# FFT layer, MLP and soft routing in one kernel: the MLP's second product replaced by turned squares, slot sums of squares and one product at the end

## The chip, the cores and the metric

The kernel runs as one program on one core of a Trainium2 chip. The metric is the device time of the whole program in microseconds (us), the median over several runs; lower is better.

## What is computed

Three layers follow one another over 8 sequences of 3072 tokens with 256 features (24576 tokens). The first filters each sequence in the frequency domain. The second is an MLP with a squared relu and 2048 hidden features. The third is a soft mixture: 32 slots, 4 for each of 8 experts, gather means over all tokens, and each token takes back a mean over the slots.

```python
# attention: X = rfft(x); Y = softshrink(X @ w + b); y = irfft(Y)
h = np.maximum(x @ w_in, 0.0)              # MLP, w_in 256 x 2048
x = h * h @ w_out                          # w_out 2048 x 256
logits = x @ phi                           # 32 slots
d = np.exp(logits - logits.max(0)); d /= d.sum(0) + 1e-09    # over the tokens
slot_input = d.T @ x
slot_out[e] = np.maximum(slot_input[e] @ w1[e], 0.0) @ w2[e]
c = np.exp(logits - logits.max(1)); c /= c.sum(1) + 1e-09    # over the slots
out = c @ slot_out
```

The MLP's output x is used in two places only, the logits and slot_input.

## The kernel before

**The front** (the loop over h that calls first_stage, b_mm, l_mm and c_mm) runs the FFT layer in units u = 0, 1, ... 95 and writes its result to DRAM (zd). Beside it runs decode(), a generator: the MLP's weights come as float64, and 32 pieces of 256 KB are loaded (raw, on the DMA queue of SyncE, SP), turned into float32 by VectorE, ScalarE and GpSimd (v, L389 and L391), and split into a part in fp32r (hi) and the remainder (lo). The loop takes one step of decode() for each h after 16, a second one when h is a multiple of 6, and at u = 80 it takes all that are left in one go (drain, L614).

**The MLP stage** has 32 steps s of 768 tokens, two halves of 384 (TOK). Its input is computed by stage_d(s+1), a generator that runs beside step s: two fills (psY, L442), each of 64 narrow float32 matmuls, then copies and splits (yh, yl). A step has 8 units q, each for 256 hidden features: a unit does seven products by Strassen's scheme as Winograd wrote it, so that four blocks (2 feature blocks a, 2 token halves c; k = 2a + c) come of seven products j and not eight. Each product is three fp32r matmuls of 128x384 (hi*hi, hi*lo, lo*hi, L658) on one of the two PSUM banks psA and psX. ScalarE copies intermediate sums away (r1, V and W, L664), VectorE adds them (h, L669) and squares (g).

The second product belongs to the unit before (prev): second(k), for each of the four blocks, multiplies the square, split again into gh and gl, by w_out, 24 matmuls of 128x384 in a unit (mm3, L116 to L118) on four banks psO that add up over the 8 units of a step:

```python
for m in range(2):
    mm3(po[m, c][:, :TOK], wo[q][:, 0, a, d], wo[q][:, 1, a, d], h, l, ...)
```

evac_o copies psO to xm, the MLP's output with features on partitions.

**The routing** is done by route(r) for a pair of steps, a generator of its own: logits (pl, L731), running maximum nn and factor al (the sums so far are multiplied by al when a larger maximum comes), exponentials e, 24 transposes of xm (px, L739) and six of the scores (py, L749), the means over slots (over_slots), slot sums (pz, L755: 12 float32 matmuls of 256 columns) which are added to acc by VectorE (L829), and a table of weights for the output (pc, co, stored to cd).

**The order of the work** is written out by hand: each engine executes its instructions as the loop issues them (manual_schedule). In a unit, beside(k) stands at four places and takes a step of stage_d where the slot 4q + k is in plan, and a step of route where it is in pairs:

```python
u.product(u.a, 0, True); r1 = u.copy("r1"); u.product(u.x, 1, True); u.add(0, r1)
prev.second(0); ...; u.square(0); beside(0)
u.product(u.a, 5, False); v = u.copy("V"); u.product(u.x, 6, True)
prev.second(3); ...; beside(1)
u.product(u.a, 4, False); u.add(3, u.copy("W")); prev.second(2); ...; beside(2)
u.product(u.a, 2, False); ...; u.product(u.x, 3, False); u.add(2, v)
prev.second(1); beside(3)
```

**The end**: in the last step the buffers of the MLP's weights become free, and loads of the experts' weights follow (load_w1 in free_wo and free_wi). Then come the logits and slot sums of the last step, the combination of the sums over the partitions (p_m, p_s, p_si), the experts (ph L1048, p2o L1066), their output by slots (pso, L1088) and the output stage, which writes the result.

## Time and profile before

| | |
|---|---|
| time, median of 3 runs | 2807.98 us (2805.99 to 2808.20) |
| the profiled execution | 2806.21 us, of which the trace's span is 2804.1 us |
| mean granted clock of TensorE | 0.989 |
| TensorE (PE) busy | 2746.1 us, 98% |
| VectorE (DVE) busy | 2049.3 us, 73% |
| ScalarE (ACT) busy | 1686.6 us, 60% |
| GpSimd (POOL) busy | 178.4 us, 6% |
| moved by DMA | 190.46 MB, mean 68 GB/s |

Busy is the time in which an engine had an instruction at work; matmuls overlap, so that the next one starts before one has ended, and a duration of a matmul is longer than the time that it keeps TensorE from the next. PEld is TensorE's loading of weights, which runs beside its matmuls. A row of the timeline joins successive instructions of one line: start, time to the last end, engine, line, operation, output and inputs, shapes, count. An idle time before an instruction stands in brackets with what ended it.

### The profile page before, as it was taken

How to read it: one execution, taken by the hardware profiler on the slowest of the kernel's cores; microseconds unless marked ns; L12 is line 12 of the kernel's file. 1: busy time of each engine (PE TensorE's matmuls, PEld its weight loads, DVE VectorE, ACT ScalarE, POOL GpSimd, SP SyncE). 2: the span in 40 equal slices, each digit the busy share in tenths (PEclk: the TensorE clock that was granted, in tenths of full speed). 3: DMA queues.
4: the chain of work that ended last, by engine and by line, in shares of the span. 5: the costliest groups of instructions: out<-in, count | busy, mean ns of one | idle time of the engine just before them, and what ended most of it. 6: DMA issues, size and time to landing. Idle time of an engine off the chain costs nothing.

```text
span 2804.1 us, 53515 instructions
## 1 busy us (share of the span) xinstructions
PE 2746.1 (98%) x21255; PEld 2571.1 (92%) x21255; DVE 2049.3 (73%) x4166; ACT 1686.6 (60%) x3720; POOL 178.4 (6%) x236
## 2 busy tenths in 40 slices
PE   7999999999999999999999999999999999999995
PEld 4788879899999999999999999999999999999974
DVE  3677777677777777777777777777777777777764
ACT  2677776566565656565656565656565656565643
POOL 0355441000000000000000000000000000000000
PEclk8999999999999999999999999999999999999997
DMA  8998986300000000000000000000100000000169
GB/s 238 250 247 239 247 218 157 68 12 12 15 13 15 12 15 12 15 12 15 12 15 13 15 12 15 12 15 12 22 12 19 12 15 12 15 12 4 38 236 381
DMA packets 99338, 190.46 MB, mean 68 GB/s; under 512 B 10928, under 2 KB 71728, under 8 KB 93072
## 3 DMA queue, kind: packets, MB, share of 16 engines
q1 hardware_dynamic: 97920, 183.86, 24.0%
q8 instruction: 167, 2.74, 0.4%
q10 hardware_dynamic: 1168, 3.18, 0.3%
q14 instruction: 83, 0.68, 0.1%
HBM read 108.36 MB, written 78.64 MB: 67 GB/s over the span
## 4 chain that ended last, share of the span: by engine, by line
PE 94%; DMA 3%; DVE 1%; issue 1%; SPq 0%; ACT 0%; POOL 0%; ACTq 0%; DVEq 0%; POOLq 0%
PE psA L658 20%; PE psX L658 14%; PE psO L118 13%; PE psO L116 13%; PE psO L117 13%; PE psB L243 3%; PE psC L327 3%; PE psY L442 2%; PE psA L210 2%; PE psL L116 2%; PE psL L117 1%; PE psL L118 1%; PE px L739 1%; DMA out_dram<-ob 1%; PE pz L755 1%; PE pl L731 1%
## 5 line engine op out<-in xcount | busy, mean ns | idle before, releaser
L118 PE MATMUL psO<-gh,wo 128*128 128x384 f32 x2048 | 684.6, 334 | 0.0
L116 PE MATMUL psO<-gh,wo 128*128 128x384 f32 x2048 | 684.0, 334 | 0.0
L117 PE MATMUL psO<-gl,wo 128*128 128x384 f32 x2048 | 684.0, 334 | 0.0
L698 DVE TENSOR_TENSOR gl<-g,gh 128x384 fp32r<-128x384 f32 x1024 | 558.0, 552 | 87.0 <-ACT gh L681 72.9
L116 PEld LDWEIGHTS psO<-gh,wo 128*128 128x128 f32 x2048 | 384.4, 188 | 0.0
L117 PEld LDWEIGHTS psO<-gl,wo 128*128 128x128 f32 x2048 | 384.4, 188 | 0.0
L118 PEld LDWEIGHTS psO<-gh,wo 128*128 128x128 f32 x2048 | 384.4, 188 | 0.0
L658 PE MATMUL psA<-yh,wia 128*128 128x384 f32 x1024 | 350.5, 342 | 0.6 <-ACT W L664 0.6
L658 PE MATMUL psA<-yh,wib 128*128 128x384 f32 x1024 | 350.1, 342 | 0.0
L658 PE MATMUL psX<-yh,wia 128*128 128x384 f32 x1024 | 342.8, 335 | 3.0 <-ACT sc L337 3.0
L669 DVE TENSOR_TENSOR h<-psX,r 128x384 f32<-128x384 f32 x256 | 142.7, 558 | 220.3 <-PE psX L658 215.5
L690 DVE SCALAR_TENSOR_TENSOR g<-h 128x384 f32<-128x384 f32 x512 | 281.8, 550 | 0.1
L664 ACT COPY r<-psA 128x384 f32<-128x384 f32 x256 | 123.4, 482 | 261.0 <-PE psA L658 261.0
L669 DVE TENSOR_TENSOR h<-psX,W 128x384 f32<-128x384 f32 x256 | 142.8, 558 | 184.9 <-ACT W L664 183.3
L674 ACT ACTIVATE r<-psA 128x384 f32<-128x384 f32 x256 | 126.2, 493 | 249.2 <-PE psA L658 249.2
L681 ACT CAST gh<-g 128x384 fp32r<-128x384 f32 x512 | 263.4, 514 | 14.5 <-DVE g L690 12.3
L692 DVE TENSOR_TENSOR g<-r 128x384 f32<-128x384 f32 x512 | 260.2, 550 | 0.1
L683 ACT ACTIVATE gh<-r 128x384 fp32r<-128x384 f32 x512 | 240.7, 518 | 8.1
L664 ACT COPY W<-psA 128x384 f32<-128x384 f32 x256 | 123.4, 482 | 202.7 <-PE psA L658 202.7
L658 PEld LDWEIGHTS psA<-yh,wia 128*128 128x128 f32 x1024 | 192.2, 188 | 13.3 <-issue 10.3
L664 ACT COPY V<-psA 128x384 f32<-128x384 f32 x256 | 123.0, 480 | 126.1 <-PE psA L658 126.1
L658 PEld LDWEIGHTS psX<-yh,wia 128*128 128x128 f32 x1024 | 192.5, 188 | 3.6 <-ACT sc L337 3.3
(213 smaller groups left out, 5091.4 us busy)
## 6 DMA issues: line engine op xcount, KB each, us to landing
bt<-ad SPq DMA_DIRECT2D x96, 256.0 KB, 4.8
zd<-sc SPq DMA_DIRECT2D x96, 256.0 KB, 4.5
zt<-zd SPq DMA_DIRECT2D x64, 384.0 KB, 6.0
xt<-in_x_dram SPq DMA_DIRECT2D x126, 192.0 KB, 4.2
ad<-sa SPq DMA_DIRECT2D x112, 192.0 KB, 4.2
out_dram<-ob SPq DMA_DIRECT2D x21, 1024.0 KB, 19.5
w<-in_moe_w_dram SPq DMA_DIRECT2D x5, 1024.0 KB, 12.6
raw<-in_moe_w_in_dram SPq DMA_DIRECT2D x16, 256.0 KB, 4.8
```

Source lines behind the costliest of these rows:

```text
L116: nc.tensor.matmul(o, lhsT=ah, rhs=bh, start=start, stop=False)
L117: nc.tensor.matmul(o, lhsT=ah, rhs=bl, start=False, stop=False)
L118: nc.tensor.matmul(o, lhsT=al, rhs=bh, start=False, stop=stop)
L658: nc.tensor.matmul(p, lhsT=w[:, k, l], rhs=r[:, j], start=start and n == 0, stop=n == 2, skip_group_check=True)
L664: nc.scalar.copy(t, self.a)
L669: nc.vector.tensor_tensor(out=h, in0=self.x, in1=t, op=ALU.add)
L674: nc.scalar.activation(out=t, in_=self.g[k].pop() if k in self.g else self.a, func=AF.Relu)
L681: nc.scalar.copy(h, self.g[k][0])
L683: nc.scalar.activation(out=h, in_=self.g[k][0], func=AF.Square)
L690: nc.vector.scalar_tensor_tensor(out=g, in0=t, scalar=0.0, in1=t, op0=ALU.max, op1=ALU.mult)
L692: nc.vector.tensor_tensor(out=g, in0=t, in1=t, op=ALU.mult)
L698: nc.vector.tensor_tensor(out=l, in0=g, in1=f(h), op=ALU.subtract)
```

## The change

The product by w_out is taken out of the loop. The squares g of a unit are kept as they are (float32).

- **Logits.** decode() computes pw = w_out phi (2048 x 32) in the front: it stores the float32 w_out to DRAM (wod), transposes the piece (pv), copies it (vt), multiplies by phi (pw) and copies the result. Unit.logits() multiplies pw by the four squares, four float32 matmuls of 32x384 in four column groups of the bank ls, which adds up over the step's units.
- **Turned squares.** Unit.turn(k) transposes a square in three pieces of 128 tokens (psT), and ScalarE copies them into one of 18 granules, in memory that w_out's pieces had (wg) and a new tile (gt).
- **Slot sums.** gather(s, i), for the unit nine places back, multiplies the granules of that unit by the exponentials ee of its step, 12 float32 matmuls of 32x128 in four column groups (into_slots), and VectorE adds the result to acc, which is now 8 blocks of 128 columns, one for each q.
- **Routing by step.** route(s) runs in step s + 1: copy of the scores (scores), sum over the two feature halves by a product with psum2 and the maximum (highest), exponentials, their transposes (weights), total, and the table for the output (rows).
- **The end.** load_wo reads w_out back in step 31; after the last slot sums acc is combined (p_f), multiplied by w_out (p_d) and folded (p_si). Eight of the loads of w1 stand behind the last slot sums now (load_w1(wg[:, k])); free_wo is gone.
- psX has two banks (fresh takes the next), psO none; ls has one and psT, for turns and gathers, two; stage_d has three more yields, so that its steps lie elsewhere, and starts at slot 6 in every step.

```diff
-    wia, wib, wo = [], [], []
+    wia, wib = [], []
+    GR = 3 * 2 * 128
+    wg = wpool.tile([128, 8, 4 * DM], F32, tag="wg", name="wg")
+    wgf = wg.rearrange("p k n -> p (k n)")
+    pw = wgf[:, 10 * GR:10 * GR + 32 * NF].rearrange("p (k n) -> p k n", n=32)
...
             if k:
-                split(wo[q][:, 0], wo[q][:, 1], v, nc.gpsimd)
+                nc.sync.dma_start(out=wod[:, 2 * q:2 * q + 2], in_=v)
+                p = pbank(f"pv{q}").rearrange("p (a d n) -> p a d n", a=2, d=2)
+                for o in range(2):
+                    for dh in range(2):
+                        nc.tensor.transpose(p[:, o, dh], in_=v[:, o, 128 * dh:128 * dh + 128], identity=ident)
+                yield
+                vt = dec.tile([128, 5, 128], F32, tag="s", name=f"vt{q}")[:, :4].rearrange("p (a d) n -> p a d n", a=2)
+                nc.scalar.copy(vt, p)
+                yield
+                p = pbank(f"pw{q}")[:, :64].rearrange("p (a n) -> p a n", a=2)
+                for o in range(2):
+                    for dh in range(2):
+                        nc.tensor.matmul(p[:, o], lhsT=vt[:, o, dh], rhs=phi[:, dh], start=dh == 0, stop=dh == 1)
+                yield
+                nc.scalar.copy(pw[:, 2 * q:2 * q + 2], p)
...
                 nc.scalar.copy(yf[2 * g + dh], ps[g])
+                yield
+            if dh == 0:
                 yield
...
+        lgp = psL.tile([128, 512], F32, tag="l", name="ls")[:, :TOK]
+        NG = 18
+        own = wk.tile([128, NG - 10, GR], F32, tag="gt", name="gt")
+        acc = rt.tile([128, NW, 128], F32, tag="acc", name="acc")
+        nc.vector.memset(acc, 0.0)
...
+        def granule(n, a):
+
+            i = (2 * n + a) % NG
+            t = wgf[:, GR * i:GR * i + GR] if i < 10 else own[:, i - 10]
+            return t.rearrange("p (b q n) -> p b q n", b=2, q=NQ)
...
+            def turn(self, *ks):
+
+                for k in ks:
+                    a, c = divmod(k, 2)
+                    p = psT.tile([128, 512], F32, tag="t", name=f"psT{self.n}_{k}")[:, :TOK].rearrange(
+                        "p (q n) -> p q n", q=NQ)
+                    for j in range(NQ):
+                        nc.tensor.transpose(p[:, j], in_=self.g[k][:, 128 * j:128 * j + 128], identity=ident)
+                    nc.scalar.copy(granule(NW * self.s + self.q, a)[:, c], p)
+
+            def logits(self):
+
+                for k in range(4):
+                    a, c = divmod(k, 2)
+                    o = 32 * (2 * c + a)
+                    nc.tensor.matmul(lgp[o:o + 32], lhsT=pw[:, 2 * self.q + a], rhs=self.g[k], start=self.q == 0,
+                                     stop=self.q == NW - 1, skip_group_check=True)
...
+        def into_slots(s, i, p):
+
+            for q in range(NQ):
+                for c in range(2):
+                    for a in range(2):
+                        o = 32 * (2 * c + a)
+                        nc.tensor.matmul(p[o:o + 32], lhsT=ee[s][:, q, c], rhs=granule(NW * s + i, a)[:, c, q],
+                                         start=q == 0, stop=q == NQ - 1, skip_group_check=True)
+
+        def gather(s, i):
+
+            p = psT.tile([128, 512], F32, tag="t", name=f"pz{s}_{i}")[:, :128]
+            into_slots(s, i, p)
+            nc.vector.scalar_tensor_tensor(out=acc[:, i], in0=acc[:, i], scalar=al[s], in1=p, op0=ALU.mult, op1=ALU.add)
...
+        def scores(s):
+            lw[s] = mid([128, TOK], "lw", s)
+            nc.scalar.copy(lw[s], lgp)
+
+        def highest(s, p):
+            p = p[:, :TOK]
+            nc.tensor.matmul(p, lhsT=psum2, rhs=lw[s], start=True, stop=True)
+            bx = small([128, 1], "bx", s)
+            no, nn = nm[s % 3], nm[(s + 1) % 3]
+            nc.vector.tensor_reduce(out=bx, in_=p, axis=AX.X, op=ALU.max)
...
+        def weights(s, p):
+            p = turn_rows(ew.pop(s), p)
+            ee[s] = rt.tile([128, NQ, 2, 32], F32, tag="ee", name=f"ee{s}", bufs=2)
+            nc.vector.tensor_copy(ee[s], p[:, :, :, 0])
...
+            p = turn_rows(lw.pop(s), p)
+            lt = rt.tile([128, NQ, 64], F32, tag="lt", name=f"lt{s}")
+            nc.vector.tensor_reduce(out=lt.rearrange("p q (b n) -> p q b n", b=2), in_=p.rearrange("p q b a n -> p q b n a"),
+                                    axis=AX.X, op=ALU.add)
...
+        def load_wo():
+            ts = [f(yp[0].tile([128, 7, TOK], F32R, tag=t, name=f"wo_{t}").rearrange("p a n -> p (a n)")) for t in ("yh", "yl")]
+            h = NF // 2
+            for k, t in enumerate(ts):
+                t = t[:, :h * DM].rearrange("p (k d) -> p k d", d=DM)
+                nc.sync.dma_start(t, wod[:, h * k:h * k + h])
...
-        pairs = [(6, 7, 9, 10, 12, 14, 15, 17, 18, 20, 21, 23, 24, 25, 26, 27, 28, 29), (9, 11, 12, 13, 19, 22)]
-        plan = set(range(25))
+        turns = (2, 3, 4, 5, 8, 13, 15, 17, 19, 21, 23, 25, 27)
+        plan = set(range(26))
...
+                if s > 0 and slot == turns[0]:
+                    side["r"] = route(s - 1, bank)
+                if s > 0 and slot in turns:
                     next(side["r"], None)
+                if s == NSB - 1 and slot == 8:
+                    load_wo()
...
             if u:
                 u.product(u.a, 0, True)
                 r1 = u.copy("r1")
-                u.product(u.x, 1, True)
+                u.product(u.fresh(0), 1, True)
                 u.add(0, r1)
             if prev:
-                prev.second(0)
-                prev.relu(2)
-                prev.hi(2)
-                prev.square(2)
-                prev.hi(1)
-                prev.square(1)
+                prev.turn(0)
             if u:
                 u.square(0)
                 beside(0)
                 u.product(u.a, 5, False)
                 v = u.copy("V")
-                u.product(u.x, 6, True)
+                u.product(u.fresh(1), 6, True)
             if prev:
-                prev.lo(2)
-                prev.second(3)
+                prev.turn(3)
             if u:
-                u.hi(0)
-                u.lo(0)
                 beside(1)
                 u.product(u.a, 4, False)
-                u.add(3, u.copy("W"))
+                w = u.copy("W")
             if prev:
-                prev.lo(1)
-                prev.second(2)
-                if prev.q == NW - 1:
-                    evac_o(prev.s, 0)
+                prev.logits()
+            if n > NW and n - 9 < NW * (NSB - 1):
+                gather(*divmod(n - 9, NW))
             if u:
+                u.add(3, w)
                 u.square(3)
                 beside(2)
                 u.product(u.a, 2, False)
                 u.relu(1)
-                u.hi(3)
                 u.product(u.x, 3, False)
+                u.square(1)
                 u.add(2, v)
-                u.lo(3)
+                u.square(2)
             if prev:
-                prev.second(1)
+                prev.turn(1, 2)
                 if prev.s == NSB - 1:
-                    free_wo(prev.q)
-                if prev.q == NW - 1:
-                    evac_o(prev.s, 1)
+                    free_wi(prev.q)
             if u:
                 beside(3)
-                if s == NSB - 1:
-                    free_wi(q)
...
+        pz = [psT.tile([128, 512], F32, tag="t", name=f"pz_{h}").rearrange("p (i n) -> p i n", n=128) for h in range(2)]
+        for i in range(4):
+            into_slots(s, i, pz[0][:, i])
...
+        for i in range(4, NW):
+            into_slots(s, i, pz[1][:, i - 4])
+        for k in range(8):
+            load_w1(wg[:, k])
...
+        lt = rows(s, bank("pr_z"))
+        p = bank("p_f").rearrange("p (i n) -> p i n", n=64)
+        for i in range(NW):
+            nc.tensor.matmul(p[:, i], lhsT=acc[:, i], rhs=mean, start=True, stop=True)
+        sf = [full(t, f"sf_{t}", 1)[:, :256].rearrange("p (i a n) -> p i a n", a=2, n=32) for t in ("V", "W")]
+        for h, copy in enumerate((nc.vector.tensor_copy, nc.scalar.copy)):
+            copy(sf[h].rearrange("p i a n -> p i (a n)"), p[:, 4 * h:4 * h + 4])
+        p = bank_x("p_d")
+        for n in range(NF):
+            i, a = divmod(n, 2)
+            c = n % 4
+            nc.tensor.matmul(p[32 * c:32 * c + 32, :DM], lhsT=sf[i // 4][:, i % 4, a], rhs=wof[n], start=n < 4, stop=n >= NF - 4,
+                             skip_group_check=True)
+        sd = full("r1", "sd", 1)[:, :DM]
+        nc.vector.tensor_copy(sd, p[:, :DM])
+        p = bank_x("p_si")
+        for dh in range(2):
+            nc.tensor.matmul(p[:, 32 * dh:32 * dh + 32], lhsT=sd[:, 128 * dh:128 * dh + 128], rhs=same[:, :32],
+                             start=True, stop=True)
+        nc.vector.tensor_copy(si, p[:, :64].rearrange("p (a s) -> p a s", a=2))
```

The lines of the changed kernel lie some 37 below (L658 is L695, L669 is L706).

**The order on TensorE** in a unit, from the end of product 4 (wib, third part) to the start of the next products; psO, psA and psX are banks, gh and gl the split squares, wia and wib the weights. Before:

```order
L658 MATMUL psA_6_14277<-yh_12793,wib_826 128x384
L116 MATMUL psO_00_13772<-gh_5_2_14297,wo_824 128x384
L117 MATMUL psO_00_13772<-gl_5_2_14324,wo_824 128x384 [waits DVE_49]
L118 MATMUL psO_00_13772<-gh_5_2_14297,wo_824 128x384
L116 MATMUL psO_10_13776<-gh_5_2_14297,wo_824 128x384
L117 MATMUL psO_10_13776<-gl_5_2_14324,wo_824 128x384
L118 MATMUL psO_10_13776<-gh_5_2_14297,wo_824 128x384
L658 MATMUL psA_6_14277<-yh_12793,wia_825 128x384 [waits Activation_49]
L658 MATMUL psA_6_14277<-yl_12794,wia_825 128x384
L658 MATMUL psA_6_14277<-yh_12793,wia_825 128x384
L658 MATMUL psX_6_14278<-yh_12793,wia_825 128x384 [waits DVE_49]
```

Now:

```order
L695 MATMUL psA_3_12846<-yh_11848,wib_806 128x384
L738 MATMUL ls<-g_2_0_12742,wg 32x384
L738 MATMUL ls<-g_2_1_12829,wg 32x384
L738 MATMUL ls<-g_2_2_12833,wg 32x384 [waits DVE_49]
L738 MATMUL ls<-g_2_3_12785,wg 32x384
L759 MATMUL pz_2_12896<-gt,ee_12631 32x128 [waits PE_49]
L759 MATMUL pz_2_12896<-gt,ee_12631 32x128 x11
L695 MATMUL psA_3_12846<-yh_11848,wia_805 128x384 [waits Activation_49]
L695 MATMUL psA_3_12846<-yl_11849,wia_805 128x384
L695 MATMUL psA_3_12846<-yh_11848,wia_805 128x384
L695 MATMUL psX_3_1_12871<-yh_11848,wia_805 128x384 [waits DVE_49]
```

The six matmuls by w_out are gone; the logits of the unit before (ls) and a gather (pz), which waits on a semaphore of TensorE, stand in their place. Product 3 (psX) waits for VectorE before and now.

**The order on VectorE** around h of block 3 (add(3), which reads psX and W). Before:

```order
L698 TENSOR_TENSOR gl_6_0_10924<-g_6_0_10895,gh_6_0_10922 128x384 [waits Activation_49]
L669 TENSOR_TENSOR h_6_3_10933<-psX_6_10868,W_6_10931 128x384 [waits Activation_49]
L698 TENSOR_TENSOR gl_5_1_10935<-g_5_1_10893,gh_5_1_10891 128x384
L690 SCALAR_TENSOR_TENSOR g_6_3_10943<-h_6_3_10933 128x384 [waits DVE_49]
L669 TENSOR_TENSOR h_6_2_10956<-psX_6_10868,V_6_10909 128x384 [waits PE_49]
L698 TENSOR_TENSOR gl_6_3_10958<-g_6_3_10943,gh_6_3_10951 128x384 [waits Activation_49]
```

Now:

```order
L766 SCALAR_TENSOR_TENSOR acc<-acc,al_15045,pz_2_15332 128x128 [waits PE_49]
L706 TENSOR_TENSOR h_3_3_15346<-psX_3_1_15307,W_3_15326 128x384 [waits Activation_49]
L720 SCALAR_TENSOR_TENSOR g_3_3_15348<-h_3_3_15346 128x384 [waits DVE_49]
L470 TENSOR_TENSOR yl_15097<-yf_0_15098,yh_15096 128x384
L718 TENSOR_TENSOR g_3_1_15359<-r_3_1_15354 128x384 [waits Activation_49]
L706 TENSOR_TENSOR h_3_2_15361<-psX_3_1_15307,V_3_15305 128x384 [waits PE_49]
L720 SCALAR_TENSOR_TENSOR g_3_2_15363<-h_3_2_15361 128x384 [waits DVE_49]
```

The update of acc, which waits for TensorE, stands ahead of h 3, and the subtractions that make gl are gone.

**The order on TensorE in the front** at u = 80, where the rest of decode() is taken: psS, psB and psL are products of the FFT layer. Before:

```order
L118 MATMUL psS_5857<-lwh_87,Sl_5833 128x256 [waits Pool_49]
L116 MATMUL psS_5857<-lwh_87,Sh_5832 128x256
L117 MATMUL psS_5857<-lwl_90,Sh_5832 128x256
L118 MATMUL psS_5857<-lwh_87,Sl_5833 128x256
L243 MATMUL psB_5892<-bm,bt_5724 128x2x64 [waits DVE_49]
L243 MATMUL psB_5892<-bm,bt_5724 128x2x64 x3
L116 MATMUL psL_5897<-lwh_88,Xh_5828 128x256 [waits DVE_49]
```

Now:

```order
L119 MATMUL psS_5883<-lwl_91,Sh_5856 128x256
L120 MATMUL psS_5883<-lwh_88,Sl_5857 128x256
L408 MATMUL pv_5954<-ident,v_5928 128x128 [waits Pool_49]
L408 MATMUL pv_5954<-ident,v_5928 128x128
L408 MATMUL pv_5954<-ident,v_5928 128x128 [waits Pool_49]
L408 MATMUL pv_5954<-ident,v_5928 128x128
L416 MATMUL pw_5961<-phi,vt_5959 128x32 [waits DVE_49,Activation_49]
L416 MATMUL pw_5961<-phi,vt_5959 128x32 x3
L248 MATMUL psB_5972<-bm,bt_5722 128x2x64 [waits PE_49]
L248 MATMUL psB_5972<-bm,bt_5722 128x2x64 x3
L118 MATMUL psL_5977<-lwh_89,Xh_5852 128x256 [waits PE_49]
```

Between psS and psB the transposes of a piece of w_out (pv) stand now, which wait for GpSimd, and the product by phi (pw), which waits for ScalarE's copy of them.

## Rows read from the trace of the kernel before

**Rows 1.** The page, part 1: engines' busy us, share of the span, instructions.
```profile
PE 2746.1 (98%) x21255; PEld 2571.1 (92%) x21255; DVE 2049.3 (73%) x4166; ACT 1686.6 (60%) x3720; POOL 178.4 (6%) x236
```

**Rows 2.** The page, part 4: the chain that ended last, by engine and by line.
```profile
PE 94%; DMA 3%; DVE 1%; issue 1%; SPq 0%; ACT 0%; POOL 0%; ACTq 0%; DVEq 0%; POOLq 0%
PE psA L658 20%; PE psX L658 14%; PE psO L118 13%; PE psO L116 13%; PE psO L117 13%; PE psB L243 3%; PE psC L327 3%; PE psY L442 2%; PE psA L210 2%; PE psL L116 2%; PE psL L117 1%; PE psL L118 1%; PE px L739 1%; DMA out_dram<-ob 1%; PE pz L755 1%; PE pl L731 1%
```

**Rows 3.** Busy time by stretch: us, engines, TensorE clock, DMA share, GB/s.
```profile
523.00:2707.00 2184.00, 2183.43 (x16600) 2124.61 (x16601) 1646.40 (x3392) 1320.51 (x2912) 0.00 (x0) 1.00 0.08 18
...
2717.00:2733.00 16.00, 15.36 (x160) 6.75 (x162) 5.55 (x15) 3.33 (x7) 0.00 (x0) 1.00 1.08 363
```

**Rows 4.** Timeline, TensorE, a plain unit's start and end: start, us, what.
```profile
1500.53 0.33 PE L658 MATMUL psA<-yh,wia 128*128 128x384 f32 x1
...
1508.15 0.34 PE L118 MATMUL psO<-gh,wo 128*128 128x384 f32 x1
1508.33 1.03 PE L739 MATMUL px<-ident,xm 128*128 128x128 f32 x8
...
1509.38 0.34 PE L658 MATMUL psA<-yl,wia 128*128 128x384 f32 x1
```

**Rows 5.** Timeline, TensorE: eight logits matmuls and the next product.
```profile
667.19 1.50 PE L731 MATMUL pl<-xm,phi 128*32 128x384 f32 x16
668.62 0.44 PE L658 MATMUL psA<-yh,wia 128*128 128x384 f32 x1
```

**Rows 6.** Timeline, TensorE: twelve slot sums and the next transposes.
```profile
749.08 1.50 PE L755 MATMUL pz<-xm,xe 128*32 128x256 f32 x24
750.51 0.55 PE L783 MATMUL pc<-ident,xe 128*128 128x128 f32 x3
```

**Rows 7.** Timeline, TensorE: a fill, and the same fill two steps later.
```profile
1543.88 0.34 PE L118 MATMUL psO<-gh,wo 128*128 128x384 f32 x1
1544.14 1.15 PE L442 MATMUL psY<-dmt,zt 48*64 48x48 f32 x64
...
1545.51 0.34 PE L658 MATMUL psA<-yl,wib 128*128 128x384 f32 x1
...
1680.98 1.15 PE L442 MATMUL psY<-dmt,zt 48*64 48x48 f32 x64
```

**Rows 8.** Groups of VectorE, MLP stage: count, busy us, mean ns, idle before.
```profile
L669 DVE TENSOR_TENSOR h<-psX,W 128x384 f32<-128x384 f32 x256 | 142.8, 558 | 184.9 <-ACT W L664 183.3
...
L829 DVE SCALAR_TENSOR_TENSOR acc<-acc,al,pz 128x256 f32<-128x256 f32 x15 | 7.1, 474 | 0.0
```

**Rows 9.** Timeline, ScalarE: r copy of the first units of steps 0, 2, and the last unit.
```profile
523.05 0.50 ACT L664 COPY r<-psA 128x384 f32<-128x384 f32 x1
...
651.72 0.48 ACT L664 COPY r<-psA 128x384 f32<-128x384 f32 x1 [1.09 <-PE psA L658]
...
2699.50 0.48 ACT L664 COPY r<-psA 128x384 f32<-128x384 f32 x1 [1.09 <-PE psA L658]
```

**Rows 10.** Groups of GpSimd, whole span.
```profile
L391 POOL TENSOR_TENSOR v<-mh,ex 128x256 f32<-128x256 f32 x32 | 26.4, 825 | 4.7 <-DVE ex L387 3.5
L389 POOL TENSOR_TENSOR mh<-mh,d 128x256 f32<-128x256 f32 x32 | 24.7, 771 | 34.6 <-ACT d L385 26.0 <-PE psS L118 8.0 <-PE psC L327 0.5
...
L122 POOL TENSOR_TENSOR wib<-s,wib 128x384 fp32r<-128x384 f32 x8 | 8.3, 1039 | 9.1 <-ACT wib L121 9.1
```

**Rows 11.** Timeline of the end: SP's queue, VectorE, TensorE.
```profile
2711.83 10.18 SPq L1021 DMA_DIRECT2D w<-in_moe_w_dram  x5
...
2717.42 0.49 DVE L1000 SCALAR_TENSOR_TENSOR acc<-acc,alz,pz_z 64x256 f32<-64x256 f32 x1
...
2717.96 0.63 PE L1036 MATMUL p_si<-mean,acc 128*128 128x32 f32 x4 [0.28 <-DVE acc L1000]
...
2718.96 1.06 PE L1048 MATMUL ph<-ea,si 128*32 128x512 f32 x8 [0.36 <-issue]
...
2736.35 1.26 PE L1088 MATMUL pso<-so,cst 128*128 128x256 f32 x4
```

254 lines of the change are left out of this document (87 added, 167 removed).

## The prediction

> **What bounds the kernel now.** I read the page first: TensorE is busy for 98% of the span [rows 1], and the chain that ended last runs through it for 94%, a third of the span in the first product (L658) and 39% in the second (L116 to L118) [rows 2]. The stretches say where: the MLP stage, 523 to 2707 us, is 78% of the span, and TensorE is busy in 2183.4 of its 2184.0 us at full granted clock, with VectorE at 75% and ScalarE at 60% [rows 3]. So a product taken out of TensorE's queue there is worth its spacing, if nothing else comes to wait. Durations mislead here, since matmuls overlap: a product shows 0.33 us, but from the first product of a plain unit at 1500.53 to the transposes that follow its 45 products at 1508.33 there are 7.80 us, **0.1733 us each** [rows 4]. A pair of steps (16 units) lasts 1680.98 - 1544.14 = 136.84 us [rows 7]: 124.8 of products, 5.1 of four fills (stage_d), and the rest routing.
>
> **Prices of what comes in.** Transposes: from the product at 1508.15 to the second after the eight transposes, at 1509.38, are 1.23 us; less two product spacings that is 0.88, or 0.110 each [rows 4]. Float32 matmuls run in two passes, and four of 32 columns each run side by side, as one set. Eight logits (16 passes, four sets of 384 columns) hold TensorE for 668.62 - 667.19 = 1.43 us [rows 5], six sets of 256 columns for 750.51 - 749.08 = 1.43 us [rows 6]. With 0.11 of each for leaving the narrow arrangement that is 0.33 and 0.22 a set (0.86 ns a column): a set of **128 columns**, which the trace does not hold, comes to 0.11 in proportion. A fill goes in 0.10 later than a product would, and the product and its successor behind it are 0.11 late each: 1.28 us in all, from 1543.88 to 1545.51 less two spacings [rows 7].
>
> **A plain unit afterwards**, along TensorE's queue (after.py's order, in us from its first product). Products 0 and 1: 1.04. turn(0), three transposes: 1.37. Products 5 and 6, turn(3): 2.74. Product 4: 3.26; into the narrow arrangement: 3.36. logits(), two sets of 384 (0.66): 4.02. gather(), six sets of 128 (0.66): 4.68. Leaving (0.22) and product 2: 5.42. Here a **new wait** stands. Product 3 accumulates on the bank that add(3) reads; VectorE's queue now has gather's acc update ahead of add(3), and that waits for gather's last pass. The last pass starts at 4.57 and ends 0.27 later, in proportion (the 24 passes of 256 columns take 1.50 to the last end, five sets and 0.02 before the last one's start, so 0.38; those of 384 likewise 0.49 [rows 5, 6]). The update (about 0.26 before the next instruction starts, estimated from L829's 0.474 for 256 columns), add(3) at 0.558 [rows 8] and two hand-overs of 0.05 (acc at 2717.42 + 0.49 to p_si at 2717.96 [rows 11]) end at 5.76. So TensorE waits 0.34. Product 3 and turn(1, 2) end the unit at **6.94**, against 7.80. Of the 24 products of the second layer (4.16 us), 3.3 are given back: 1.32 of transposes, 1.32 of logits and gather, 0.32 of arrangement changes, 0.34 of waiting.
>
> ScalarE loses four hi casts and one relu and gains four turn copies: eight instructions of about 0.48 in a unit plus the side work, near 5 us of 6.94. VectorE loses four lo subtractions and gains the acc update. Neither is a bound. But r1 now stands behind the copies of turn(1) and turn(2) and, in about half of the units, a stage_d cast; there it ends 0.1 to 0.2 after product 5 could start. I add 0.3 us a step for that.
>
> **A step afterwards**: 8 x 6.94 = 55.5; two fills 2.57 (they stand at slots 6 and 10 now); routing, per step instead of per pair: the score sum over psum2 in two passes (0.66) and nine transposes (0.99). With the 0.3: **60.0**, against 68.42 (half a pair). The old routing's 24 transposes a pair, its logits, slot sums and xm copies go. From the r copies [rows 9], steps 0 and 1 took 128.7 us and the 29 steps and 7 units from there 2047.8. Afterwards: step 0, which has no gather and so no such wait, about 50, step 1 59, then 29 x 60.0 = 1740 and 51 for the seven units: 1900 against 2176.5. **The stage gives 276.**
>
> **The front.** decode() no longer splits w_out; it stores it to DRAM (8 x 256 KB on SP, behind loads that are issued three units ahead), transposes it (4 x 0.110), copies, multiplies by phi (8 passes of 128 weight columns, 0.11 each, as the transposes) and copies again: 1.32 us of TensorE for each of eight, and TensorE has no room there: **+10.6**. Four yields more for each make 184 decode steps, but only 169 are taken up to the drain at u = 80, so 15 are issued in a block: on GpSimd the last two sums and three splits of w_in (about 4.4 us; the largest split is 1.039) and one value (0.771 + 0.825) [rows 10], then the second value through VectorE, ScalarE and GpSimd (about 4 us), then transposes, copy and product (about 2 us). TensorE's queue has those transposes ahead of everything later, so it stands for **about 13 us**; if part overlaps with earlier work, 6. Another 3 for the other seven, whose transposes wait on GpSimd. Front: **+27**, between +12 and +35.
>
> **The end.** From the last unit's r copy at 2699.50 to the slot MLP's first product at 2718.96 it was 19.5 us [rows 9, 11]: 7.1 for the rest of the unit, 4.2 of its second-layer products, 8.2 of routing. Now: 6.2, then that unit's turns, logits and gather (2.9), then one after another score copy, sum, maximum, exponentials, transposes and copy (4.6), eight sums of six sets (5.2), update, product by mean, w_out, fold and copies (7.2): 26.1, so +7. Eight loads of 512 KB that were spread over the last step now stand on SP behind those sums and ahead of the w2 loads, which begin at 2711.83 now [rows 11]; 4.2 MB at the 363 GB/s of that stretch [rows 3] are 11.6 us, of which the longer chain hides over half. The output stage starts with ro, 1.3 us after pso (2736.35 now); it is the same. **+12**, between +7 and +19. load_wo (2 MB) has all of step 31 to land.
>
> **The sum.** The profiled execution took 2806.2 (2804.1 of span and 2.1 around it), 1.8 below the median of the runs, 2808.0. 2806.2 - 276 + 27 + 12 = 2569, 2571 against the median; I give **2570**. What a measurement can tell from no change here is about 0.2%, 6 us.
>
> Bounds of the set of 128 columns: below, the fill's 16 sets of 48 columns (1.08 us less 0.11, 0.06 each); above, the set of 256, 0.22. A unit has six, 248 units have them: -74 to +164. I take the proportional value, since 256 and 384 columns agree on it.
>
> **The rivals.**
> (a) The sets do not get shorter below 256 columns: 2570 + 164 = 2734. For it: the narrow loads of weights show 0.11 us each. Against it: the fills, whose sets are at 0.06. 7%.
> (b) TensorE waits for ScalarE at both round trips that a turn stands in (r1 to product 5, V to product 4), half a microsecond a unit: +128, so 2700. For it: each is covered by 0.33 of transposes where 1.04 of second products stood. Against: ScalarE is idle a quarter of the time. 13%.
> (c) Slower: **transposes one after another**. If each held TensorE for its duration instead of its spacing (eight show 1.03 us from first start to last end with 0.11 between starts, so 0.26 each [rows 4]), twelve would cost 1.9 us more a unit, 256 x 1.9 = 490: 3060. The point from which it decides is a spacing of 0.187 (238 us over 256 x 12). For it: every turn starts on squares from VectorE and a bank that ScalarE must have emptied, unlike the eight in a row. Against: the spacing seen, and that the squares are a unit old. 3%.
> The Trainium skill (TensorE: Matmul & The Clock Gate, Part 4: PE-mode transpose) speaks against the change here: it gives about 275 ns for a 128x128 transpose in a kernel, where transposes do not hold the full clock. By 275 ns in sequence, the 3072 transposes would cost 845 us instead of 338, an estimate from that page that would put the time near 3080. This trace agrees on the duration and not on the cost.
> (d) The change does not remove what it says: the 6144 second-layer products are gone from the order of TensorE, so under 1%.
>
> **Chances.** Forecast 76%, within 2530 to 2640; (a) 7, (b) 13, (c) 3, unnamed 1. The range must leave out no more than 2 in 10: down to 2530 (a short drain, short sets), up to 2660, into (b). Faster by over 0.2%: 0.95, within: 0.01, slower: 0.04.
>
> **What would show it.** Right: first products of plain units 6.9 us apart, steps 60; product 3 idle 0.3 on VectorE's h; gather's 24 passes 0.65 apart from end to end; psT transposes 0.11 apart; a hole of 10 us or more before u = 81 in the front, released by GpSimd; pso some 12 us later after the last unit. Wrong: units over 7.3, product 5 idle on ScalarE in most units, or a granted clock below 1.00 between the front and the output.

## The result, and the profile after

The changed kernel takes **2622.61 us** (median of 4 runs, 2622.13 to 2623.41) against 2807.93 us before in the same comparison: a ratio of 0.9342, 95% interval 0.9325 to 0.9358, 185 us faster. The prediction was 2570 (2530 to 2660): the right side and inside the range, with 52 us of the forecast gain missing. The profiled execution took 2623.41 us, of which 2621.6 is the trace's span.

The page of the changed kernel: busy time by engine (part 1), and the chain that ended last by engine and by line (part 4).

```profile
PE 2503.3 (95%) x25694; PEld 2026.2 (77%) x25694; DVE 1690.7 (64%) x3523; ACT 1480.2 (56%) x3356; POOL 169.7 (6%) x228
...
PE 84%; DVE 7%; DMA 4%; issue 1%; SPq 1%; ACT 1%; POOL 0%; DVEq 0%; POOLq 0%; ACTq 0%
PE psA L695 19%; PE psX L695 17%; PE psT L730 13%; PE ls L738 8%; PE pz L759 7%; DVE h L706 3%; PE psB L248 3%; PE psC L332 3%; PE psY L462 3%; DVE acc L766 2%; PE psA L215 2%; PE psL L118 2%; PE psL L119 2%; PE psL L120 2%; DMA out_dram<-ob 1%
```

Against [rows 1, 2], VectorE now has 7% of the chain where it had 1%. The products by w_out (39%) are gone; turns (psT), logits (ls) and gathers (pz) took 28%.

The r copies of the same units as in [rows 9], on ScalarE:

```profile
549.49 0.48 ACT L701 COPY r<-psA 128x384 f32<-128x384 f32 x1 [0.56 <-PE psA L695]
...
2497.71 0.48 ACT L701 COPY r<-psA 128x384 f32<-128x384 f32 x1
```

With these and pso (2553.88 now, 2736.35 before [rows 11]) the span falls into four stretches:

| stretch, us | before | after | change | predicted |
|---|---|---|---|---|
| start to the first r copy (front) | 523.05 | 549.49 | +26.4 | +27 |
| first to last r copy (MLP stage) | 2176.5 | 1948.2 | -228.2 | -276 |
| last r copy to pso (end) | 36.9 | 56.2 | +19.3 | +12 |
| pso to the end of the span | 67.8 | 67.7 | 0 | 0 |

The front came out as forecast, the end 7 us longer, and the stage gave 48 us less. So the stage is where to look. One unit of it on TensorE (timeline: start, time to the last end, what), from product 0 to the next unit's product 0:

```profile
1499.94 0.42 PE L695 MATMUL psA<-yh,wia 128*128 128x384 f32 x1
...
1501.07 0.49 PE L730 MATMUL psT<-ident,g 128*128 128x128 f32 x3
1501.43 0.45 PE L695 MATMUL psA<-yh,wib 128*128 128x384 f32 x1
1501.72 0.34 PE L695 MATMUL psA<-yl,wib 128*128 128x384 f32 x1
...
1502.61 0.49 PE L730 MATMUL psT<-ident,g 128*128 128x128 f32 x3
1502.92 0.44 PE L695 MATMUL psA<-yh,wib 128*128 128x384 f32 x1
...
1503.64 0.85 PE L738 MATMUL ls<-g,wg 128*32 128x384 f32 x8
1504.31 0.84 PE L759 MATMUL pz<-gt,ee 128*32 128x128 f32 x24
1505.07 0.45 PE L695 MATMUL psA<-yh,wia 128*128 128x384 f32 x1
1505.36 0.34 PE L695 MATMUL psA<-yl,wia 128*128 128x384 f32 x1
1505.53 0.33 PE L695 MATMUL psA<-yh,wia 128*128 128x384 f32 x1
1506.08 0.44 PE L695 MATMUL psX<-yh,wia 128*128 128x384 f32 x1 [0.21 <-DVE h L706]
1506.36 0.33 PE L695 MATMUL psX<-yl,wia 128*128 128x384 f32 x1
...
1506.70 0.82 PE L730 MATMUL psT<-ident,g 128*128 128x128 f32 x6
1507.28 0.42 PE L695 MATMUL psA<-yh,wia 128*128 128x384 f32 x1
```

**The prices hold.** Transposes in a turn are 0.109 us apart: after turn(1, 2), six of them from 1506.70, product 0 comes at 1507.28 and the next matmul at 1507.53. The logits take 1504.31 - 1503.64 = 0.67 us (0.66 forecast), the 24 passes of gather and the step out of the narrow arrangement, to the second matmul of product 2, 1505.36 - 1504.31 = 1.05 (0.66 + 0.22 + a product spacing of 0.17 forecast).

**The waits do not.** Undisturbed, the second matmul of a product comes 0.35 us after the last matmul of the product before it, or 0.29 after the last transpose. Product 3 begins at 1506.08, 0.55 after the last matmul of product 2 (1505.53) and not 0.17, and its second comes another 0.28 later (1506.36): 0.83 in all, **0.48 lost**, where 0.34 was forecast. The queue on VectorE is the forecast one: acc's update, and h behind it.

```profile
1505.21 0.35 DVE L766 SCALAR_TENSOR_TENSOR acc<-acc,al,pz 128x128 f32<-128x128 f32 x1 [1.66 <-PE pz L759]
1505.48 0.55 DVE L706 TENSOR_TENSOR h<-psX,W 128x384 f32<-128x384 f32 x1
```

And two products wait that were forecast to wait little or not at all: product 5 (1501.43, on ScalarE's r1, which stands behind an ACTIVATE of the routing, lt) and product 4 (1502.92, on V). In the following unit r1 stands behind the copies of turn(1, 2) and a cast of stage_d (yh), the case that the prediction named; here ScalarE, then TensorE.

```profile
1507.23 0.86 ACT L731 COPY gt<-psT 128x384 f32<-128x384 f32 x2 [0.77 <-PE psT L730]
1507.98 0.52 ACT L467 CAST yh<-yf 128x384 fp32r<-128x384 f32 x1
1508.39 0.49 ACT L701 COPY r<-psA 128x384 f32<-128x384 f32 x1
```

```profile
1508.41 0.49 PE L730 MATMUL psT<-ident,g 128*128 128x128 f32 x3
1508.93 0.44 PE L695 MATMUL psA<-yh,wib 128*128 128x384 f32 x1
1509.21 0.34 PE L695 MATMUL psA<-yl,wib 128*128 128x384 f32 x1
```

r1 ends at 1508.88, product 5 starts at 1508.93 behind three transposes that began at 1508.41, and its second matmul is at 1509.21: 0.59 after the last transpose (1508.62), 0.30 lost.

Over steps 2 to 30 of the trace, a step loses 1.1 us at product 5 (late in units 2, 3, 5 and 6, by 0.14 to 0.30; over all eight units the mean is 0.42, where 0.29 is undisturbed), 0.6 at product 4 (units 1, 4 and 5) and 2.9 at product 3 (six units of 0.48; in the two with a fill behind the gather the fill covers it). Steps are **61.5 us** apart where 60.0 was forecast. Units without a fill or a product of the routing take 7.17 to 7.35 where 6.94 was forecast, so that the prediction's own sign of being wrong, "units over 7.3", is there in part.

The page's groups (busy, mean ns, idle before, releaser) show little of this: 40.9 us of idle time at product 3, and 2.1 at products 5 and 4 together, since a matmul that is held for 0.38 us counts as idle only for 0.21 while the one before it is still at work.

```profile
L695 PE MATMUL psX<-yh,wia 128*128 128x384 f32 x1024 | 365.5, 357 | 40.9 <-DVE h L706 40.9
...
L695 PE MATMUL psA<-yh,wib 128*128 128x384 f32 x1024 | 396.3, 387 | 2.1
```

### The profile page after: what moved, and what is told of

The parts are those of the page before. It is cut to its first block, busy times and chain, and to the rows that moved or that the text cites. A ratio compares the mean times of both kernels' runs of the same rounds, so it can differ in the third digit from the quotient of the medians.

```text
span 2621.6 us, 61545 instructions
## 1 busy us (share of the span) xinstructions
PE 2503.3 (95%) x25694; PEld 2026.2 (77%) x25694; DVE 1690.7 (64%) x3523; ACT 1480.2 (56%) x3356; POOL 169.7 (6%) x228
## 4 chain that ended last, share of the span: by engine, by line
PE 84%; DVE 7%; DMA 4%; issue 1%; SPq 1%; ACT 1%; POOL 0%; DVEq 0%; POOLq 0%; ACTq 0%
PE psA L695 19%; PE psX L695 17%; PE psT L730 13%; PE ls L738 8%; PE pz L759 7%; DVE h L706 3%; PE psB L248 3%; PE psC L332 3%; PE psY L462 3%; DVE acc L766 2%; PE psA L215 2%; PE psL L118 2%; PE psL L119 2%; PE psL L120 2%; DMA out_dram<-ob 1%
## 5 line engine op out<-in xcount | busy, mean ns | idle before, releaser
L730 PE MATMUL psT<-ident,g 128*128 128x128 f32 x3072 | 460.1, 272 | 0.2 <-ACT wg L731 0.2
L720 DVE SCALAR_TENSOR_TENSOR g<-h 128x384 f32<-128x384 f32 x768 | 428.8, 558 | 26.4
L695 PE MATMUL psX<-yh,wia 128*128 128x384 f32 x1024 | 365.5, 357 | 40.9 <-DVE h L706 40.9
L730 PEld LDWEIGHTS psT<-ident,g 128*128 128x128 f32 x3072 | 382.3, 140 | 28.1 <-ACT wg L731 0.5
L695 PE MATMUL psA<-yh,wia 128*128 128x384 f32 x1024 | 399.8, 390 | 2.9 <-ACT sc L342 2.2
L695 PE MATMUL psA<-yh,wib 128*128 128x384 f32 x1024 | 396.3, 387 | 2.1
L731 ACT COPY wg<-psT 128x384 f32<-128x384 f32 x576 | 262.5, 482 | 165.7 <-PE psT L730 159.6
L731 ACT COPY gt<-psT 128x384 f32<-128x384 f32 x448 | 204.2, 482 | 127.7 <-PE psT L730 123.5
L695 PEld LDWEIGHTS psX<-yh,wia 128*128 128x128 f32 x1024 | 192.3, 188 | 100.8 <-DVE h L706 100.3
L695 PEld LDWEIGHTS psA<-yh,wia 128*128 128x128 f32 x1024 | 192.3, 188 | 52.3 <-issue 31.1
L695 PEld LDWEIGHTS psA<-yh,wib 128*128 128x128 f32 x1024 | 192.3, 188 | 44.5 <-ACT r L701 25.1
L738 PE MATMUL ls<-g,wg 128*32 128x384 f32 x2048 | 218.3, 498 | 0.0
L695 PE MATMUL psX<-yh,wib 128*128 128x384 f32 x512 | 174.0, 340 | 0.0
L695 PE MATMUL psA<-yl,wib 128*128 128x384 f32 x512 | 172.7, 337 | 0.0
L695 PE MATMUL psA<-yl,wia 128*128 128x384 f32 x512 | 172.4, 337 | 0.0
L695 PE MATMUL psX<-yl,wia 128*128 128x384 f32 x512 | 172.3, 337 | 0.0
L706 DVE TENSOR_TENSOR h<-psX,r 128x384 f32<-128x384 f32 x256 | 141.7, 554 | 43.4 <-PE psX L695 16.5
L701 ACT COPY W<-psA 128x384 f32<-128x384 f32 x256 | 122.6, 479 | 57.1 <-PE psA L695 47.9
L706 DVE TENSOR_TENSOR h<-psX,W 128x384 f32<-128x384 f32 x256 | 141.0, 551 | 12.5 <-ACT W L701 12.5
```

Of the source, the lines that this page charges most:

```text
L695: nc.tensor.matmul(p, lhsT=w[:, k, l], rhs=r[:, j], start=start and n == 0, stop=n == 2, skip_group_check=True)
L701: nc.scalar.copy(t, self.a)
L706: nc.vector.tensor_tensor(out=h, in0=self.x, in1=t, op=ALU.add)
L720: nc.vector.scalar_tensor_tensor(out=g, in0=t, scalar=0.0, in1=t, op0=ALU.max, op1=ALU.mult)
L730: nc.tensor.transpose(p[:, j], in_=self.g[k][:, 128 * j:128 * j + 128], identity=ident)
L731: nc.scalar.copy(granule(NW * self.s + self.q, a)[:, c], p)
```

## The experiments

All kernels below are the changed kernel with edits. Each time is the median of 4 or 5 runs, made beside the kernel before in one of four comparisons. The median of the kernel before was 2806.5 to 2808.1 us in them, so that differences of 2 us between kernels of different comparisons mean nothing; the runs of one kernel lie up to 13 us apart (experiment 10). The ratio, with its 95% interval, is to the kernel before; the changed kernel's is 0.9342. A side step is what one call of beside(k) issues: the next piece of stage_d, of the routing, or of both. The table has units and steps in us, medians over steps 2 to 29:

| kernel | units 0 to 7 | step |
|---|---|---|
| changed | 7.62 8.49 8.03 7.73 7.35 7.35 7.73 7.17 | 61.5 |
| update behind (1) | 7.13 8.48 8.03 7.25 6.87 6.88 7.27 6.70 | 58.6 |
| fourth side step later (2) | 7.17 8.95 7.95 7.42 7.35 7.35 7.43 7.17 | 60.8 |
| three moves (3) | 6.69 9.24 7.75 6.97 6.65 6.66 6.97 6.70 | 57.6 |
| four moves (4) | 6.69 8.71 7.73 6.97 6.65 6.65 6.97 6.70 | 57.1 |

### 1. The update of acc behind the square of block 3

```diff
             if n > NW and n - 9 < NW * (NSB - 1):
-                gather(*divmod(n - 9, NW))
+                pz = gather(*divmod(n - 9, NW))
             if u:
                 u.add(3, w)
                 u.square(3)
+            if n > NW and n - 9 < NW * (NSB - 1):
+                gathered(*pz)
```

(gather now only returns its bank, and gathered holds VectorE's update alone.)

> The changed kernel with one thing moved: VectorE's update of acc behind the addition and the square of block 3, so that product 3 no longer stands behind a gather. Theory: in the changed kernel's trace the second matmul of product 3 starts 0.84 us after the last of product 2 in 6 of 8 units of a step (0.35 undisturbed), and in the two units with a fill, which covers it, 0.35. 186 units by 0.49 us is 91 us, some of which later waits take back: 2622 - 85 = 2537 us, and product 3 waits no more. Rival: the addition is late because of ScalarE's copy W, not of the update: no change, 2622. Second rival: the last turn's bank, which the gather shares, now comes free later, and half of it is lost there: 2580.

Measured: 2532.93 us, ratio 0.9022 (0.9010 to 0.9035), **90 us faster** than the changed kernel. VectorE, and TensorE's third matmul of product 2 and product 3:

```profile
1516.13 0.56 DVE L706 TENSOR_TENSOR h<-psX,W 128x384 f32<-128x384 f32 x1 [0.56 <-ACT W L701]
...
1517.19 0.34 DVE L769 SCALAR_TENSOR_TENSOR acc<-acc,al,pz 128x128 f32<-128x128 f32 x1
```

```profile
1517.35 0.34 PE L695 MATMUL psA<-yh,wia 128*128 128x384 f32 x1
1517.52 0.33 PE L695 MATMUL psX<-yh,wia 128*128 128x384 f32 x1
1517.69 0.33 PE L695 MATMUL psX<-yl,wia 128*128 128x384 f32 x1
```

h now follows W and ends at 1516.69, before the gather is done; the update comes after. Product 3 follows product 2 at 0.17 us and its second matmul at 0.17. Every unit without a fill is shorter by 0.46 to 0.49, the two with one are unchanged. Both rivals fall.

### 2. The fourth side step behind r1

```diff
                 u.product(u.a, 0, True)
                 r1 = u.copy("r1")
+            if prev:
+                beside(3, prev.s, prev.q)
+            if u:
                 u.product(u.fresh(0), 1, True)
...
-            if u:
-                beside(3)
             prev = u
```

(beside takes the unit's s and q as arguments now.)

> The changed kernel with the fourth side step of a unit (stage_d's or the routing's) issued behind the next unit's copy r1 instead of ahead of it. Theory: ScalarE takes r1 late because a cast of stage_d stands ahead of it; the second matmul of product 5 starts 0.45 to 0.59 us after the last transpose in four of eight units, 0.29 undisturbed, 1.1 us a step in all. 0.8 of it goes: 31 by 0.8 is 25 us, 2597. Rival: it is the copies of the two turns that make r1 late: no change.

Measured: 2598.62 us, ratio 0.9257 (0.9244 to 0.9270), 24 us faster. The two turn copies and r1 on ScalarE:

```profile
1506.21 0.86 ACT L731 COPY wg<-psT 128x384 f32<-128x384 f32 x2 [0.78 <-PE psT L730]
1507.11 0.48 ACT L701 COPY r<-psA 128x384 f32<-128x384 f32 x1
```

r1 follows the turn copies at once, and product 5's second matmul is 0.29 to 0.32 behind the transposes in every unit. The rival falls. But only 0.7 us a step is won: the side steps' copies and casts that stood ahead of r1 stand ahead of V now, and product 4's second matmul comes 0.51 to 0.54 after the transposes in units 2 and 5, where it had been at 0.30 and 0.37. (Unit 0 is shorter and unit 1 longer by 0.45 because the product for the scores, pl, now stands on the other side of the border between them.)

### 3. Three moves: the update, the fourth and the first side step

Experiments 1 and 2, and:

```diff
-                beside(0)
                 u.product(u.a, 5, False)
                 v = u.copy("V")
+                beside(0)
```

> Three moves together on the changed kernel: the update of acc behind the square of block 3, the fourth side step behind the next unit's r1, and the first side step behind the copy V. Theory: the first is worth 90 us as measured alone (2533); the second took 1.1 us a step from product 5, but 0.45 came back at product 4, since a cast then stood ahead of V (the second matmul of product 4 came 0.51 to 0.54 after the transposes in two more units). With V ahead of it both go, 1.1 and 0.5 us a step: 2533 - 31 x 1.6 = 2483, and no product is later than 0.30 behind transposes. Rival: the casts then stand ahead of the copies of the turns and W instead, and half comes back: 2510.

Measured: 2503.29 us, ratio 0.8922 (0.8908 to 0.8936); 30 us less than experiment 1, not 50. Products 5 and 4 are undisturbed (0.29 to 0.33 in all units), as forecast. Plain units take 6.65 to 6.70. But unit 1 takes 9.24. There the routing's exponentials come behind V on ScalarE, and the transposes of them wait on TensorE:

```profile
1703.18 0.48 ACT L701 COPY V<-psA 128x384 f32<-128x384 f32 x1
1703.55 0.59 ACT L823 ACTIVATE e<-pl,nm 128x384 f32<-128x384 f32 x1
```

```profile
1704.29 0.55 PE L750 MATMUL py<-ident,e 128*128 128x128 f32 x3 [0.34 <-ACT e L823]
```

py starts 0.61 us after the last transpose of the turn (1703.68), 0.50 late. The rival named the wrong place: not casts and turn copies, but a chain of the routing itself, one side step of which feeds the next.

### 4. Four moves: the second side step too

```diff
-                beside(1)
                 u.product(u.a, 4, False)
                 w = u.copy("W")
+                beside(1)
```

> The three moves of the side steps and the update, and the second side step too: behind product 4 and the copy W. With three moves the second unit of a step took 9.24 us, where it had taken 8.48: the transposes of the exponentials (py) stood 0.5 us for ScalarE's e, which now comes behind V. Theory: with product 4 between them e is ready; the second unit takes 0.5 to 0.7 us less, 31 x 0.6 = 18 us: 2503 - 18 = 2485. Rival: the gather behind it then waits for ee (VectorE's copy of py) and takes it all back: 2503.

Measured: 2484.40 us, ratio 0.8849 (0.8836 to 0.8862), 19 us less. On TensorE, unit 1:

```profile
1464.03 0.34 PE L695 MATMUL psA<-yh,wib 128*128 128x384 f32 x1
1464.21 0.49 PE L750 MATMUL py<-ident,e 128*128 128x128 f32 x3
1464.63 0.53 PE L738 MATMUL ls<-g,wg 128*32 128x384 f32 x4
```

py follows product 4 at 0.18 us, and unit 1 takes 8.71 in place of 9.24; the gather behind does not wait, so the rival falls.

### 5 and 6. decode() without the block at u = 80

The front's block in the changed kernel, TensorE's rows with their idle time, and the stretches around it (columns as in [rows 3]):

```profile
461.36 0.69 PE L408 MATMUL pv<-ident,v 128*128 128x128 f32 x2 [8.08 <-POOL v L396]
465.05 0.69 PE L408 MATMUL pv<-ident,v 128*128 128x128 f32 x2 [3.00 <-POOL v L396]
466.41 1.92 PE L416 MATMUL pw<-phi,vt 128*128 128x32 f32 x8 [0.68 <-ACT vt L411]
```

```profile
460.00:473.00 13.00, 7.96 (x35) 7.17 (x36) 2.86 (x8) 2.88 (x7) 2.83 (x4) 0.50 0.15 46
473.00:480.00 7.00, 7.00 (x56) 6.33 (x56) 4.12 (x8) 3.60 (x9) 1.12 (x2) 0.94 0.35 79
```

The holes are 8.08 + 3.00 + 0.68 us. A second cost, which the prediction did not have: in the 13 us from 460 TensorE was granted 0.50, the level of 1.2 GHz; it had stood from 453.3 to 461.4. From u = 80 to 88 (the start of psB) it took 53.9 us instead of 35.7 before: +18. Experiment 5:

```diff
-                for _ in range(1 + (h % 6 == 0)):
+                for _ in range(1 + (h % 3 == 0)):
                     next(dec_run, None)
```

> The changed kernel with two steps of decode() at every third h instead of every sixth, so that all 184 are taken before u = 80 and nothing is left for the block there. Theory: the holes of 8.1, 3.0 and 0.7 us go and with them the 8 us at half clock that follow (about 4 us lost): -15 us, 2607. Rival: the same work of GpSimd then delays TensorE in small pieces, so that the front stays as long: 2622.

Measured: 2616.38 us, ratio 0.9323 (0.9308 to 0.9337): 6 us less, though the intervals overlap. The trace shows both theory and rival: the block is gone (35.9 us from u = 80 to 88), but from u = 56 to 64 it takes 47.6 instead of 40.7, with a hole like the old ones:

```profile
351.81 0.69 PE L408 MATMUL pv<-ident,v 128*128 128x128 f32 x2 [4.02 <-POOL v L396]
```

Experiment 6 (whose expectation gives another place for the block; it lies between u = 80 and 88) takes two steps at every second h and puts a yield between v and its transposes:

```diff
-                for _ in range(1 + (h % 6 == 0)):
+                for _ in range(1 + (h % 2 == 0)):
...
                 nc.sync.dma_start(out=wod[:, 2 * q:2 * q + 2], in_=v)
+                yield
```

> The changed kernel with two steps of decode() at every second h, and one more yield between GpSimd's last product of a piece of w_out and its transposes. Theory: with two steps at every third h the block at u = 80 was gone (18 us between the 64th and the 72nd group of psB), but 7 us came back at 346 to 352 us, where transposes were issued in the same h as the GpSimd product that they wait for and TensorE stood 4.0 us. With a yield between them that hole goes too: 2610. Rival: GpSimd simply is too busy at twice the pace and the holes stand elsewhere: 2616 as with every third h, or worse.

Measured: 2607.74 us, ratio 0.9294 (0.9277 to 0.9311): 15 us less than the changed kernel. No hole at pv is left. From u = 56, 64, 72 and 80 eight units each take 41.6, 41.5, 38.2 and 35.9 us in place of 40.7, 40.7, 39.0 and 53.9, 17 us less. The profiled execution took 2615.11 us: from u = 8 to 24 it needed 92.8 us, where the changed kernel's needed 82.7, and TensorE was granted 0.50 in parts of that stretch.

### 7 to 9. The loads at the end

The chain of the changed kernel at the end (start, us, what), and SP's queue:

```profile
2519.70 5.07 DMA wg<-in_moe_w_dram
...
2524.78 3.78 SPq L1050
...
2528.60 4.27 SPq L1050
...
2532.91 2.92 SPq L1050
...
2535.88 12.20 DMA w<-in_moe_w_dram
...
2548.12 5.83 PE p2o L1088 x58
```

```profile
2517.69 4.98 SPq L869 DMA_DIRECT2D wg<-in_moe_w_dram  x8
...
2523.36 15.43 SPq L1050 DMA_DIRECT2D w<-in_moe_w_dram  x5
```

From the landing of the first w1 (wg) on, the chain is the queue: eight loads of w1 that wait for the slot sums, five of w2 behind them, and TensorE's p2o at last waits for w2 until 2548.12. Experiment 7 leaves the eight out, so that the last experts compute with whatever lies in that memory; it serves for the time alone:

```diff
-            load_w1(wg[:, k])
+            ew1[divmod(len(ew1), 2)] = wg[:, k]
```

> The changed kernel without the eight loads of w1 at the end (the slot MLP of the last experts reads what is left in that memory). Theory: from the first of the last 64 matmuls of p2o to pso it takes 12.7 us in the changed kernel and 4.0 before; the w2 loads wait behind these eight on the queue. Without them 4 to 5 us: -8 us, 2614. Rival: the w2 loads are late by themselves, since they start 5 us before they did in relation to the first ph: no change.

Measured: 2613.21 us, ratio 0.9311 (0.9298 to 0.9324), 9 us less. From the last r copy to pso it takes 46.9 us instead of 56.2, and the first w2 load is issued 7.3 us after that copy (2500.22), where it was 25.7:

```profile
2507.54 12.70 SPq L1050 DMA_DIRECT2D w<-in_moe_w_dram  x5
```

Experiment 8 issues two of the eight before and six amid the slot sums, whose order is turned so that their memory comes free sooner; 9 issues all eight behind w2 (the two lines of the loop over load_w1 moved behind the loop that issues w2, the order of the sums as it was). The diff of 8:

```diff
+        for k in (6, 7):
+            load_w1(wg[:, k])
         for i in range(4):
-            into_slots(s, i, pz[0][:, i])
+            into_slots(s, 4 + i, pz[1][:, i])
+        for k in range(6):
+            load_w1(wg[:, k])
...
-        for i in range(4, NW):
-            into_slots(s, i, pz[1][:, i - 4])
-        for k in range(8):
-            load_w1(wg[:, k])
+        for i in range(4):
+            into_slots(s, i, pz[0][:, i])
```

> The changed kernel with the last eight slot sums in another order: units 4 to 7, which lie in the memory that w1 is loaded into, first, then units 0 to 3; two of the eight loads are issued before the sums, six between them, where all eight stood behind. Nothing else moves. The loads can start some 4 us earlier, two of them 10 us earlier. Theory: the w2 loads, and with them the second half of p2o, are late because the queue is full of w1; they land 4 to 6 us earlier, 2617. Rival: the early loads only take the place of others (the DMA engines are the bound from the first load to the last): no more than 2 us, 2621.

> The changed kernel with the eight loads of w1 issued behind the five loads of w2 instead of ahead of them. Without the eight loads the w2 loads were issued at 2507.5, 8 us after the last unit's first copy, and not 10 us after the last slot sum's start. Theory: SP's queue is what holds them: the eight wait for the slot sums at its head, and w2, whose memory is free, stands behind. In the other order w2 lands during the slot sums and w1 behind it, before its experts' turn: nearly all of what leaving the loads out gave, -8 us, 2614. Rival: the bytes are the bound (9.4 MB at some 363 GB/s are 26 us), and now w1 is late instead: -2 us at most.

Measured: 8 takes 2618.57 us (0.9328, 0.9316 to 0.9341), 9 takes 2617.00 (0.9323, 0.9310 to 0.9337). Both intervals overlap the changed kernel's, so the medians alone settle nothing; in the traces the stretch from the last r copy to pso is 51.8 and 52.8 us instead of 56.2. From the slot MLP's first product (ph) to pso it takes 26.8 us in the changed kernel, 17.4 without the eight loads (experiment 7), 18.7 in 8 and 20.6 in 9. In 8 no product waits for w1 or w2 any more (the 18.7 stand at a granted clock of 0.93, the 17.4 at 1.00), so from ph on the loads had cost time by their place in the queue and not by their bytes. In 9, with w2 ahead, an expert's first product waits for its w1.

```profile
2533.85 1.06 PE L1070 MATMUL ph<-wg,si 128*32 128x512 f32 x8 [1.51 <-DMA wg<-in_moe_w_dram]
```

A part of what 8 and 9 win is lost ahead of that: ph starts 33.1 and 32.2 us after the last r copy, and 29.4 in the changed kernel. TensorE's granted clock differs there. Between these two points it is 0.84 on average in 8 and in 9, and 0.94 in the changed kernel. Experiment 10 below has the order of 8, and its profile shows 1.00: there it is 28.2 us to ph and 17.4 from ph to pso. Whether the orders of 8 and 9 bring the lower clock with them is not shown; experiment 11 has the order of 8 too, and 0.83.

### 10 to 12. Together

> All moves together: the three of the side steps and the update, two steps of decode() at every second h with the yield, and the other order of the last slot sums. Theory: they lie in different stretches and add up: 2483 - 12 - 5 = 2466. Rival: they add up only where each alone held: 2500.

> The same four moves with two steps of decode() at every second h, the yield, and the other order of the last slot sums. Theory: 18 us less than with three moves: 2482 - 18 = 2464. Rival: no change, 2482.

> The four moves, two steps of decode() at every second h and the yield, with this order of the loads instead of the other order of the last slot sums. Theory: 2465 + 4 - 8 = 2461. Rival: w1 late, 2467.

Measured: three moves with experiments 6 and 8 (10), 2481.87 us (0.8847, 0.8832 to 0.8862), between its theory and its rival, as experiment 3 had been; four moves with 6 and 8 (11), **2464.76 us** (0.8774, 0.8763 to 0.8786); four moves with 6 and 9 (12), 2468.64 us (0.8796, 0.8781 to 0.8810), nearer to its rival. The intervals of the last two overlap, and of the 8.7 us between their profiled spans 6.3 lie in the front, whose code is the same in both; so they do not decide between 8 and 9. The moves lie in different stretches and add up. The best is 158 us faster than the changed kernel and also beats the kernel before.

## Why the prediction was right, and where it was not

- **What bounds it: right.** TensorE's queue bounds the stage before and after, and work taken out of it was worth its spacing: without waits a plain unit takes 6.65 us (experiment 4), and the prediction's sum less its 0.34 of waiting is 6.60.
- **The set of 128 columns: right.** It was taken in proportion at 0.11 us, with 0.06 and 0.22 as ends; successive sets of a gather start 0.109 us apart in the trace. Rival (a) falls.
- **Product 3's wait: right in its mechanism, too small and too many.** Forecast 0.34 in eight units, found 0.48 in six. The hole itself (0.38) was close; what lacked is that the matmul after a held one comes 0.28 later and not 0.17. In the two units of a step with a fill, wait and fill were both counted, though the fill stands between the gather and product 3 and covers the wait. So this term alone was off by only 0.2 us a step (2.9 for 2.7), by luck, since the two errors nearly cancel. Taking the wait away gave 90 us (experiment 1).
- **The step that failed: "I add 0.3 us a step for that".** Product 5 was late in half of the units, as the text said, but by 0.14 to 0.30 us and not by 0.1 to 0.2: 1.1 us a step. (Four units at 0.1 to 0.2 would already have made 0.4 to 0.8, not 0.3.) Another 0.6 were lost at product 4, where V came late and for which nothing was set. Rival (b) had just this mechanism, half a microsecond in every unit; it came in part, 0.2 a unit. That is 0.8 and 0.6 us more than forecast, with product 3's 0.2 together 1.6 a step where 1.5 was found. By the r copies (the first of step 2 is at 661.96) steps 0 and 1 took 112.5 us where 109 was set, and the rest 1835.8 where 1791 was: 3.5 and 45, the stage's 48. Of the 3.5, step 0 has 2.3, which no run explains. The text asked whether ScalarE was busy (about 5 us of 6.9, "not a bound"), where it mattered what stands ahead of one copy. Experiments 2 to 4 show it, since moving the side steps, with the same work, took it away (58.6 to 57.1 us a step beyond experiment 1).
- **Rival (c): wrong.** The transposes of a turn show 0.27 us each and are 0.109 apart. (From the prediction's own 0.26 and 0.11 the rival's price is 1.8 us a unit, not 1.9, and its time 3030; it falls all the same.) The Trainium skill (TensorE: Matmul & The Clock Gate, Part 4: PE-mode transpose) gives about 275 ns for a 128x128 transpose in a kernel, beside a figure for bf16; here they are float32. The trace agrees on the duration, 272 ns here, and not on the cost, since 3072 of them hold TensorE for 109 ns each, at a granted clock of 1.00 from 555 to 2510 us.
- **The front: right in sum, by two errors.** +26.4 for +27. Up to u = 80 it was 9.1 us (psB at 449.7 against 440.6), where 10.6 for work and 3 for waits were set; the block was +18.2 and not 13, as the half clock came on top.
- **The end: +19.3 for +12.** The chain to the slot MLP's first product is 29.4 us after the last r copy (19.5 before [rows 9, 11]), 3 more than forecast. The eight loads cost 9.3 where the longer chain was to hide over half of 11.6. The text named their place ahead of the w2 loads, but priced their bytes alone: they wait for the slot sums at the head of the queue, so that the w2 loads start 25.7 us after the last r copy (12.3 before [rows 9, 11]).
